# A chunk-select attention and gMLP kernel whose scheduler gets another length model, with the k copies as max(x,x) and the identity made first

## The chip, the core and the metric

The kernel runs on one core of a Trainium2 chip. The metric is the device time of one execution in microseconds (us). Five engines work side by side, each through its own list in order: TensorE (PE; its weight loads are PEld), VectorE (DVE), ScalarE (ACT), GpSimd (POOL) and SyncE (SP). Here GpSimd issues all loads and SyncE all stores and all crossbar transposes; a transfer then runs on the core's 16 DMA engines. An engine that waits for something holds up everything behind it in its list.

## The reference

Inputs are q, k, v of (4, 8, 768, 64) and the weights of one gated MLP. For every query the 6 best of 24 chunks of 32 keys are chosen by an upper bound, attention runs over these chunks, and the joined heads go through the MLP with a spatial mix:

```python
k_min, k_max = min and max of k over each chunk of 32 keys
ub = sum(maximum(q * k_min, q * k_max))        # per query and chunk, causal
top_chunks = argsort(ub)[-6:]
scores = q @ k.T / 8, masked to top_chunks and causal
x = softmax(scores) @ v                        # heads joined: (4, 768, 512)
h = relu(x @ w_in);  u, v = h[..., :512], h[..., 512:]
v_n = (v - mean(v)) / sqrt(var(v) + 1e-6)
v_s = w_spatial @ v_n + b_spatial
out = (u * v_s) @ w_out
```

## The kernel before

The work is cut into 16 pairs of heads (4 batches of 4 pairs) and, after each batch's four pairs, the MLP of that batch in 6 tiles of 128 rows. Matmuls run on f16 with f32 sums in 8 banks of PSUM.

For a pair: GpSimd loads kp, qs (two halves) and vt (L321, L325, L328), casting to f16. TensorE transposes k (L376) and ScalarE copies it to kT. VectorE makes chunk minima and maxima of kT (L382, L385, L388: a tree) into kmm, spreads them into km (L395: on VectorE for pairs 0 and 1, on GpSimd after) and copies kT into kh (L403, four copies of 64x384 that change between the two partition halves). q is transposed (L410) and its positive and negative parts are rq (L412, L415); L425 multiplies rq by km, which gives the bounds. VectorE masks them (L433), finds the 8 largest (L441) and writes "not chosen" flags into spare columns of qs (L447). qs with its flags is transposed into a: by TensorE (L461, copied by L464) for pairs 0 to 4, by a crossbar transpose that SyncE issues (L452) from pair 5 on. The flags meet large negative rows in kh (the pattern ex, made from identity at L292 and copied by six L300 copies into three kh buffers), so that one score matmul (L486) also masks. ScalarE takes exp (L493), GpSimd zeroes the upper triangle from pair 4 on (L501), L510 multiplies by v, L518 and L522 normalize into x. x is transposed into xT: on TensorE (L538, L541) for pairs 0 to 3 and the last, by SyncE (L530) for the others.

For a tile of the MLP: v = L557 on xT, ScalarE's relu (L561), bn_stats and bn_aggr on VectorE (L563, L565), normalization (L574); u = L584 and L588; the spatial sum L598 over six tiles of v; g = L602; g transposed to gT by SyncE (L606) in batches 0 to 2 and by TensorE (L613, L615) in batch 3; L620 multiplies by w_out; ScalarE copies to o (L623) and SyncE stores it (L625).

Nothing of this order is written by hand. Every step is an op with an engine, a length (occ), a time after which others see its result (vis), a key and the buffers that it reads and writes. Schedule.run plays the ops through: it always takes the op that can start first by its model, with the smaller key where two tie, gives it a PSUM bank and notes it. That sequence is then issued, so the numbers in the model decide each engine's list. Loads pass one model server (loads), everything else only its engine. The two lines on loads:

```python
loads = max(loads, t + 0.6) + o.load
o.seen = loads + 1.7
```

Of the kernel before, what the change touches and what calls it, by code (L numbers as in the profile page):

```python
# [14 lines left out]
P = 128  # L15
# [42 lines left out]
class Op:  # L58
    __slots__ = ("eng", "occ", "vis", "emit", "key", "take", "drop", "deps", "left", "users", "start", "end",
                 "seen", "load", "n", "tag")  # L60


class Schedule:
# [31 lines left out]
    def run(self):  # L95
        free = {e: 0.0 for e in ("PE", "ACT", "DVE", "POOL", "SP")}
# [19 lines left out]
        while left:  # L116
# [48 lines left out]
MM = 1 / 2400.0  # L165

# [15 lines left out]
def kernel(  # L182
# [93 lines left out]
    def const_ops():  # L276
        s.op("DVE", 0.1, 0.2, lambda: nc.vector.memset(identity, 0.0), -100, w=["identity"])
        s.op("POOL", *pool(P), c_identity, -90, w=["identity"], r=["identity"])
# [19 lines left out]
        for j in range(len(kh_r)):  # L298
            for hi in range(2):
# [33 lines left out]
    def weight_ops(key):  # L333
# [22 lines left out]
    def spatial_ops(key):  # L356
        for so in range(NQT):
# [7 lines left out]
            s.op("DVE", 0.474, 0.58, lambda so=so, bk=bk: nc.vector.tensor_copy(wsT[:, so, :], bk.f16[:, 0:S]),  # L365
# [306 lines left out]
```

## Time and profile before

| what | us |
|---|---|
| time, median of 2 runs | 238.43 (237.49 and 239.36) |
| the profiled execution's own time | 237.0 |
| its span | 235.0 |
| TensorE busy | 194.6 (83%) |
| VectorE busy | 171.9 (73%) |
| ScalarE busy | 144.6 (62%) |
| GpSimd busy | 102.9 (44%) |
| software DMA queue (loads), share of 16 engines | 71.7% |
| hardware DMA queue (stores, transposes) | 32.5% |

The span runs from the first to the last instruction that the profiler saw; the profiled execution's own time is 2 us longer. Busy time of TensorE counts each matmul to the end of its result, so it says little about how full it is; where it stood is read from its idle times and from what ended them. The share of a whole span mixes stages with different limits, so the rows below are taken by stretch.

### The profile page before, as it was taken

Reading aid. Unit: us, or ns where it says so; the run is one execution under the profiler, and the core shown is the slowest. Engines: PE = TensorE matmul, PEld = TensorE weight load, DVE = VectorE, ACT = ScalarE, POOL = GpSimd, SP = SyncE. Lnnn points to the kernel's source line nnn. Section 1 sums busy time; section 2 is a strip of 40 time slices with the busy share of each in tenths; the row PEclk is TensorE's granted clock in tenths of the full one; section 3 lists DMA queues with packets and bytes.
Section 4 is the critical chain, followed back from the end, with each engine's and each line's share of the span. In section 5 each row is a group of like instructions: output and inputs, shape, how many; then the busy total and the mean of one; then the engine's idle time right before and its main releaser. Section 6 shows DMA issues by size and latency. Waiting matters only on the chain. (4 is left out here: it accounts for less than half of the span.)

```text
span 235.0 us, 5366 instructions
## 1 busy us (share of the span) xinstructions
PE 194.6 (83%) x1910; PEld 115.8 (49%) x1910; DVE 171.9 (73%) x604; ACT 144.6 (62%) x297; POOL 102.9 (44%) x184
## 2 busy tenths in 40 slices
PE   0259889797999895794999987996999998699983
PEld 0146767576555453462655543564455554344541
DVE  4899999999899957278489994399996332276450
ACT  2117877767997833596588742797796847266111
POOL 8998579752836562194556452144310302000000
PEclk9999999999999999999799999999799999979999
DMA  9999999999893999999996979839512665100222
GB/s 60 122 150 148 155 174 189 177 134 109 60 137 35 135 175 157 230 129 109 109 162 57 96 164 143 208 134 134 79 27 42 106 181 168 45 0 0 80 101 89
DMA packets 117306, 27.68 MB, mean 118 GB/s; under 512 B 111904, under 2 KB 114208, under 8 KB 117280
## 3 DMA queue, kind: packets, MB, share of 16 engines
q0 software_dynamic: 77200, 12.19, 71.7%
q1 hardware_dynamic: 40080, 15.15, 32.5%
q8 instruction: 15, 0.25, 0.4%
q14 instruction: 11, 0.09, 0.1%
HBM read 24.38 MB, written 6.29 MB: 131 GB/s over the span
## 5 line engine op out<-in xcount | busy, mean ns | idle before, releaser
L493 ACT ACTIVATE e<-bank 128x512 f16<-128x512 f32 x192 | 93.0, 554 | 26.4 <-PE bank L486 13.6
L486 PE MATMUL bank<-a,kh 128*128 128x512 f16 (+3 forms) x256 | 58.2, 312 | 3.9 <-DVE a L464 2.1
L501 POOL TENSOR_SCALAR_AFFINE_SELECT e<-e 128x384 f16<-128x384 f16 x48 | 25.3, 529 | 69.2 <-ACT e L493 68.8
L598 PE MATMUL bank<-vn,wsT 128*128 128x512 f16 x144 | 37.2, 379 | 0.0
L623 ACT COPY o<-bank 128x512 f32<-128x512 f32 x24 | 14.0, 585 | 35.9 <-PE bank L620 34.2
L510 PEld LDWEIGHTS <-e 128*128 128x128 f16 x672 | 28.8, 98 | 10.8 <-POOL e L501 1.3
L510 PE MATMUL bank<-vt,e 128*128 128x65 f16 x672 | 32.4, 194 | 1.0 <-POOL e L501 0.6
L486 PEld LDWEIGHTS <-kh 128*128 128x128 f16 x256 | 23.0, 99 | 17.3 <-issue 3.6
L602 DVE SCALAR_TENSOR_TENSOR g<-bank,bcol,u 128x512 f16<-128x512 f32 x24 | 17.9, 748 | 17.4 <-PE bank L598 15.5
L557 PE MATMUL bank<-w_in,xT 128*128 128x512 f16 x96 | 27.7, 419 | 3.6 <-DMA xT<-x 3.0
L620 PE MATMUL bank<-w_out,gT 128*128 128x512 f16 x96 | 23.9, 380 | 7.6 <-DMA gT<-g 7.0
L325 POOL DMA_DIRECT2D qs<-in_q_dram x32 | 26.7, 848 | 2.3 <-DMA a<-qs 2.1
L584 PE MATMUL bank<-w_in,xT 128*128 128x512 f16 x96 | 24.3, 379 | 0.0
L403 DVE COPY kh<-kT 64x384 f16<-64x384 f16 x64 | 22.2, 347 | 1.2
L321 POOL DMA_DIRECT2D kp<-in_k_dram x16 | 17.0, 1064 | 9.7 <-PE bank L376 7.1
L561 ACT ACTIVATE vraw<-bank 128x512 f32<-128x512 f32 x24 | 14.0, 607 | 9.5 <-PE bank L557 9.3
L378 ACT COPY kT<-bank 128x768 f16<-128x768 f16 x16 | 13.1, 821 | 10.8 <-PE bank L376 10.0
L563 DVE BATCH_NORM_STATS2 st<-vraw 128x6 f32<-128x512 f32 x24 | 15.9, 682 | 4.8 <-ACT vraw L561 4.8
L518 DVE RECIPROCAL rec<-bank 128x6 f32<-128x6 f32 x32 | 6.0, 186 | 18.1 <-PE bank L510 17.9
L598 PEld LDWEIGHTS <-wsT 128*128 128x128 f16 x144 | 13.1, 97 | 11.9 <-issue 0.3
L522 DVE TENSOR_TENSOR x<-bank,rec 128x384 f16<-128x384 f32 x32 | 17.7, 553 | 0.6
L328 POOL DMA_DIRECT2D vt<-in_v_dram x16 | 16.5, 1034 | 3.3 <-PE bank L510 2.5
(59 smaller groups left out, 258.3 us busy)
## 6 DMA issues: line engine op xcount, KB each, us to landing
out_dram<-o SPq DMA_DIRECT2D x24, 256.0 KB, 2.3
kp<-in_k_dram POOLq DMA_DIRECT2D x16, 192.0 KB, 5.0
qs<-in_q_dram POOLq DMA_DIRECT2D x32, 96.0 KB, 4.9
vt<-in_v_dram POOLq DMA_DIRECT2D x16, 192.0 KB, 5.9
ws_raw<-in_moe_w_spatial_dram POOLq DMA_DIRECT2D x3, 384.0 KB, 8.5
w_in<-in_moe_w_in_dram POOLq DMA_DIRECT2D x4, 256.0 KB, 8.5
w_out<-in_moe_w_out_dram POOLq DMA_DIRECT2D x2, 256.0 KB, 8.3
gT<-g SPq DMA_TRANSPOSE x18, 2.5
```

The source lines that it names most:

```text
L325: s.op("POOL", 0.84, 0, lambda hi=hi, c0=c0: nc.gpsimd.dma_start(out=qs[:, :, hi, c0:c0 + D], in_=one(q, hi)), key + 0.1, w=[("qd", i % le ...
L403: nc.vector.tensor_copy(o, f)
L486: mm(bs.f32[:, col:col + n], lhsT=kh[:, hi, t * P:(t + 1) * P], rhs=af[:, q0 // P:(q0 + n) // P, :], start=True, stop=not dg)
L493: s.op("ACT", *act_cost(WIDTHS[g]), lambda g=g, bs=bs, e=e: nc.scalar.activation(out=e[:, BASES[g]:BASES[g] + WIDTHS[g]], in_=bs.f32[:, 0: ...
L501: nc.gpsimd.affine_select(out=o, in_=o, compare_op=Alu.is_ge, fill=0.0, base=0, channel_multiplier=-1, pattern=[[0, 3], [1, P]])
L510: mm(o[:, qi, :], lhsT=e[:, c:c + P], rhs=vt[:, hi, t, 0:D + 1], start=(part == 0 and n == 0), stop=(part == 1 and n == len(bl) - 1))
L522: nc.vector.tensor_tensor(x16[:, :, hi, :], in0=o[:, :, 0:D], in1=rec.to_broadcast([P, NQT, D]), op=Alu.mult)
L557: mm(bk.f32, lhsT=x[:, ko, t * P:(t + 1) * P], rhs=w_in_sb[:, ko, DH:DFF], start=(ko == 0), stop=(ko == NDO - 1))
L584: mm(bk.f32, lhsT=x[:, ko, t * P:(t + 1) * P], rhs=w_in_sb[:, ko, 0:DH], start=(ko == 0), stop=(ko == NDO - 1))
L598: mm(bk.f32, lhsT=wsT[:, si, t * P:(t + 1) * P], rhs=vn[:, si, :], start=(si == 0), stop=(si == NQT - 1))
L602: s.op("DVE", 0.61, 0.70, lambda t=t, bk=bk, g=g: nc.vector.scalar_tensor_tensor(out=g, in0=bk.f32, scalar=bcol[:, t:t + 1], in1=u_r[nu[t] ...
L620: mm(bo.f32, lhsT=gT[:, db, :], rhs=w_out_sb[:, db, :], start=(db == 0), stop=(db == KO - 1))
```

## The change

No arithmetic changes. The scheduler gets other numbers and rules:

- the engines start late by a little (free), a result is seen 0.25 later by another engine (LATE);
- an op with `load` passes the one DMA server, and now stores and crossbar transposes have a load too; a transfer of SyncE is seen 1.5 later than before (LATE_X);
- `slack`: a load can start only 3.0 after what it waits for, a store 4.0 (0.3 in the last batch), by the model. The chip's instruction waits as before; only its place in the list comes later;
- most lengths of VectorE are set anew, the kh copies from 0.16 to 0.28;
- the kh copies, and the km copies of pairs 0 and 1, are `tensor_tensor` max of x with x;
- the identity's key puts it behind the first load of GpSimd's queue.

```diff
-        free = {e: 0.0 for e in ("PE", "ACT", "DVE", "POOL", "SP")}
+        free = {"PE": 0.8, "ACT": 2.1, "DVE": 0.8, "POOL": 1.3, "SP": 0.8}
...
-                t = max(t, d.end if d.eng == o.eng == "PE" else d.seen)
-            ready[o.eng].append((o.key, o.n, t, o))
+                t = max(t, d.end if d.eng == o.eng == "PE" else d.seen if d.eng == o.eng else d.seen + LATE)
+            ready[o.eng].append((o.key, o.n, t + o.slack if o.deps else t, o))
...
-                loads = max(loads, t + 0.6) + o.load
-                o.seen = loads + 1.7
+                loads = max(loads, o.end) + o.load
+                o.seen = loads + 1.5 + (LATE_X if o.eng == "SP" else 0.0)
...
+LATE = 0.25
+LATE_X = 1.5
+LOAD_SLACK = 3.0
...
-        s.op("POOL", *pool(P), c_identity, -90, w=["identity"], r=["identity"])
+        s.op("POOL", *pool(P), c_identity, -100.99, w=["identity"], r=["identity"])
...
-                    (nc.vector if i < 2 else nc.gpsimd).tensor_copy(o, f)
+                    if i < 2:
+                        nc.vector.tensor_tensor(o, in0=f, in1=f, op=Alu.max)
+                    else:
+                        nc.gpsimd.tensor_copy(o, f)
...
-                    nc.vector.tensor_copy(o, f)
-                s.op("DVE", 0.16, 0.28, put, key + 3, r=[("kT", n2)], w=[("kh", nh, hi, par)])
+                    nc.vector.tensor_tensor(o, in0=f, in1=f, op=Alu.max)
+                s.op("DVE", 0.28, 0.40, put, key + 3, r=[("kT", n2)], w=[("kh", nh, hi, par)])
...
-            s.op("SP", 2.7, 4.7, lambda: nc.sync.dma_start_transpose(
+            s.op("SP", 1.5, 0, lambda: nc.sync.dma_start_transpose(
...
-                s.op("SP", 0.95, 3.0, lambda g=g, gT=gT: nc.sync.dma_start_transpose(out=gT, in_=g), kk,
-                     r=[("g", ng)], w=[("gT", ngt)])
+                s.op("SP", 1.25, 0, lambda g=g, gT=gT: nc.sync.dma_start_transpose(out=gT, in_=g), kk,
+                     r=[("g", ng)], w=[("gT", ngt)], load=0.55)
```

Every engine's list changes by this; the lines of the changed kernel lie 3 to 6 further down. Two places are shown.

VectorE's list at the start of the program before (kh0 to kh2 are the three kh buffers, t1 and t2 the tree, bank2 the bounds of pair 0):

```order
L300 COPY kh0_92<-ex_70 64x768
L382 TENSOR_TENSOR t10_95<-kT0_90 128x384 x2
L385 TENSOR_TENSOR t20_97<-t10_95 128x192 x2
L388 TENSOR_REDUCE kmm0_99<-t20_97 128x24 x2
L412 TENSOR_SCALAR rq0_103<-bank1_62 128x640
L395 COPY km0_101<-kmm0_99 64x2x3x4 x4
L415 TENSOR_SCALAR rq0_103<-bank1_62 128x640
L403 COPY kh0_92<-kT0_90 64x3x128 x4
L433 TENSOR_TENSOR bank2_63<-bank2_63,cmask_71 128x5x2x4
L300 COPY kh0_92<-ex_70 64x768
L441 MAX m80_105<-bank2_63 128x8 x10
L300 COPY kh1_93<-ex_70 64x768
```

The same place in the changed kernel, from the first kh<-ex copy on:

```order
L303 COPY kh0_92<-ex_70 64x768 x2
L293 MEMSET vt2_88 128x12x2
L283 MEMSET km1_102 128x48
L289 MEMSET eps_73 128x1
L303 COPY kh1_93<-ex_70 64x768 x2
L303 COPY kh2_94<-ex_70 64x768 x2
L276 MEMSET qs3_85 128x6x32
L277 MEMSET qs3_85 128x6x32
L293 MEMSET vt3_89 128x12x2
L385 TENSOR_TENSOR t10_95<-kT0_90 128x384 x2
L388 TENSOR_TENSOR t20_97<-t10_95 128x192 x2
L391 TENSOR_REDUCE kmm0_99<-t20_97 128x24 x2
```

All six copies of ex and the last memsets moved ahead of the first tree. Before, one stood ahead of it, one between mask and L441, one behind L441 and three behind the first L447.

SyncE's list in the MLP of batch 0 before (a is the transposed q of a pair, x the normalized output, o a store's tile):

```order
L530 DMA_TRANSPOSE xT1_122<-x162_120 128x6x128
L606 DMA_TRANSPOSE gT0_164<-g0_160 128x4x128
L606 DMA_TRANSPOSE gT1_165<-g1_161 128x4x128
L452 DMA_TRANSPOSE a1_108<-qs3_85 128x12x128
L625 DMA out_0_dram<-o0_170 128x512
L606 DMA_TRANSPOSE gT2_166<-g2_162 128x4x128
L530 DMA_TRANSPOSE xT1_122<-x160_118 128x6x128
L625 DMA out_0_dram<-o1_171 128x512
L606 DMA_TRANSPOSE gT3_167<-g3_163 128x4x128
L625 DMA out_0_dram<-o2_172 128x512
L606 DMA_TRANSPOSE gT4_168<-g0_160 128x4x128
```

And in the changed kernel:

```order
L612 DMA_TRANSPOSE gT0_164<-g0_160 128x4x128
L612 DMA_TRANSPOSE gT1_165<-g1_161 128x4x128
L536 DMA_TRANSPOSE xT1_122<-x162_120 128x6x128
L458 DMA_TRANSPOSE a1_108<-qs3_85 128x12x128
L612 DMA_TRANSPOSE gT2_166<-g2_162 128x4x128
L612 DMA_TRANSPOSE gT3_167<-g3_163 128x4x128
L612 DMA_TRANSPOSE gT4_168<-g0_160 128x4x128
L536 DMA_TRANSPOSE xT1_122<-x160_118 128x6x128
L631 DMA out_0_dram<-o0_170 128x512
L612 DMA_TRANSPOSE gT5_169<-g1_161 128x4x128
L458 DMA_TRANSPOSE a2_109<-qs0_82 128x12x128
```

The stores moved behind the transposes, because the L620 that make their tiles moved. How far is counted in TensorE's two lists: the matmul columns between the last L598 of a tile and the first L620 of the same tile, and between the last L510 of pair 7 and the second half of the first L557 of batch 1, in units of one 512-column matmul:

| tile | 0 | 1 | 2 | 3 | 4 | 5 |
|---|---|---|---|---|---|---|
| batch 0, before | 26.1 | 20.6 | 23.7 | 22.2 | 18.7 | 25.4 |
| batch 0, changed | 34.8 | 37.8 | 49.0 | 44.6 | 41.4 | 37.6 |
| batch 1, before | 19.9 | 28.1 | 19.6 | 24.9 | 29.9 | 19.9 |
| batch 1, changed | 31.6 | 30.8 | 31.0 | 36.9 | 37.6 | 31.5 |
| batch 2, before | 27.2 | 20.2 | 17.9 | 21.2 | 18.9 | 18.9 |
| batch 2, changed | 36.7 | 31.8 | 32.1 | 31.9 | 30.9 | 32.1 |

xT of pair 7: 17.9 before, 28.3 changed. From the K transpose of pair 11 to that of pair 14: 155.8 before, 46.6 changed.

## Rows read from the trace of the kernel before

**Rows 1.** Stretches in us: busy time (count) of each engine, clock, DMA share, GB/s.

```profile
0.00:20.00 20.00, 7.03 (x56) 5.28 (x57) 15.47 (x62) 4.10 (x6) 18.70 (x26) 1.00 1.84 116
20.00:80.00 60.00, 54.19 (x722) 38.25 (x720) 57.80 (x223) 47.13 (x99) 38.34 (x67) 1.00 1.44 132
80.00:115.00 35.00, 26.91 (x273) 15.94 (x272) 21.36 (x78) 21.15 (x43) 15.43 (x29) 0.97 1.42 157
```

**Rows 2.** The chain that ended last: start us, us, what.

```profile
215.57 2.59 PE bank L598 x12
```

**Rows 3.** Waits, TensorE: line waited for, us in total, times, longest.

```profile
PE bank L620 <- DMA gT<-g: 7.0, 8, 2.4
PE bank L557 <- DMA xT<-x: 3.0, 1, 3.0
PE bank L425 <- DVE x L522: 2.0, 1, 2.0
PE bank L425 <- POOL km L395: 1.6, 4, 0.8
```

**Rows 4.** Timeline, TensorE, 81 to 91: start us, us, what, [idle before <-releaser].

```profile
81.67 0.59 PE L598 MATMUL bank<-vn,wsT 128*128 128x512 f16 x2
...
90.53 0.82 PE L620 MATMUL bank<-w_out,gT 128*128 128x512 f16 x3 [2.42 <-DMA gT<-g]
```

**Rows 5.** Stretches of 5 us; columns as in rows 1, clock third from last.

```profile
110.00:115.00 5.00, 3.09 (x32) 2.35 (x33) 2.00 (x7) 2.20 (x5) 0.77 (x2) 0.82 1.63 154
115.00:120.00 5.00, 5.00 (x38) 2.52 (x37) 3.79 (x20) 2.48 (x6) 4.20 (x8) 0.84 1.14 91
...
165.00:170.00 5.00, 4.84 (x26) 2.35 (x25) 4.85 (x18) 4.06 (x8) 1.52 (x5) 0.72 0.60 84
```

**Rows 6.** Timeline, VectorE, 5 to 22 us.

```profile
7.23 0.63 DVE L382 TENSOR_TENSOR t<-kT 128x384 f16<-128x384 f16 x2 [0.75 <-ACT kT L378]
...
8.63 0.48 DVE L412 TENSOR_SCALAR rq<-bank 128x640 f16<-128x640 f16 x1
9.03 1.89 DVE L395 COPY km<-kmm 64x24 f16<-64x24 f16 x4
...
11.47 1.43 DVE L403 COPY kh<-kT 64x384 f16<-64x384 f16 x4
12.93 0.21 DVE L433 TENSOR_TENSOR bank<-bank,cmask 128x40 f32<-128x40 f32 x1
13.17 0.58 DVE L300 COPY kh<-ex 64x768 f16<-64x768 f16 x1
...
14.59 0.33 DVE L300 COPY kh<-ex 64x768 f16<-64x768 f16 x1
...
15.28 2.14 DVE L300 COPY kh<-ex 64x768 f16<-64x768 f16 x3
...
20.17 0.71 DVE L395 COPY km<-kmm 64x24 f16<-64x24 f16 x4
```

**Rows 7.** Single lines: count, ns min/median/max, first and last start.

```profile
L403 DVE COPY kh<-kT x64: 334/347/352, 11.5 to 171.9; 64x384 f16<-64x384 f16 x64
L382 DVE TENSOR_TENSOR t<-kT x32: 315/349/629, 7.2 to 162.8; 128x384 f16<-128x384 f16 x32
L385 DVE TENSOR_TENSOR t<-t x32: 210/248/574, 7.8 to 163.6; 128x192 f16<-128x192 f16 x32
```

**Rows 8.** Timeline, start, TensorE and GpSimd; last row: DMA issues, us to landing.

```profile
5.56 0.80 PE L376 MATMUL bank<-identity,kp 128*128 128x128 f16 x6 [5.56 <-POOL identity L269]
...
6.21 1.05 POOL L321 DMA_DIRECT2D kp<-in_k_dram  x1
...
kp<-in_k_dram POOLq DMA_DIRECT2D x16, 192.0 KB, 5.0
```

**Rows 9.** Timeline, GpSimd and VectorE, 158.5 to 161 us.

```profile
159.56 0.52 POOL L501 TENSOR_SCALAR_AFFINE_SELECT e<-e 128x384 f16<-128x384 f16 x1 [0.36 <-ACT e L493]
...
159.62 0.74 DVE L385 TENSOR_TENSOR t<-t 128x192 f16<-128x192 f16 x2
```

More of the change, by code (lines that the diff above doesn't have):

```diff
@@ L59 @@
     __slots__ = ("eng", "occ", "vis", "emit", "key", "take", "drop", "deps", "left", "users", "start", "end",
-                 "seen", "load", "n", "tag")
+                 "seen", "load", "slack", "n", "tag")
 class Schedule:
@@ L69, in __init__, with op @@
         self.writer, self.readers = {}, {}
-    def op(self, eng, occ, vis, emit, key, r=(), w=(), take=None, drop=None, load=0.0, tag=""):
+    def op(self, eng, occ, vis, emit, key, r=(), w=(), take=None, drop=None, load=0.0, slack=0.0, tag=""):
         o = Op()
         o.eng, o.occ, o.vis, o.emit, o.key, o.take, o.drop = eng, occ, vis, emit, key, take, drop
-        o.load, o.n, o.tag = load, len(self.ops), tag
+        o.load, o.slack, o.n, o.tag = load, slack, len(self.ops), tag
         deps = set()
@@ L93, in op, with run @@
         return o
-    def run(self):
-        free = {e: 0.0 for e in ("PE", "ACT", "DVE", "POOL", "SP")}
+    def run(self, fixed=None):
+        free = {"PE": 0.8, "ACT": 2.1, "DVE": 0.8, "POOL": 1.3, "SP": 0.8}
         ready = {e: [] for e in free}
@@ L364, in spatial_ops @@
                  take=bk, w=[bk])
-            s.op("DVE", 0.474, 0.58, lambda so=so, bk=bk: nc.vector.tensor_copy(wsT[:, so, :], bk.f16[:, 0:S]),
+            s.op("DVE", 0.48, 0.60, lambda so=so, bk=bk: nc.vector.tensor_copy(wsT[:, so, :], bk.f16[:, 0:S]),
                  key + 0.1 * so, r=[bk], w=[("wsT", so)], drop=bk)
@@ L381, in prep_ops @@
         for m, op in ((0, Alu.max), (1, Alu.min)):
-            s.op("DVE", 0.26, 0.38, lambda m=m, op=op: nc.vector.tensor_tensor(
+            s.op("DVE", 0.28, 0.40, lambda m=m, op=op: nc.vector.tensor_tensor(
                 t1[:, m], in0=kc[:, :, 0:16], in1=kc[:, :, 16:32], op=op), key, r=[("kT", n2)], w=[("t1", n2, m)])
@@ L434, in add_mask @@
                 [P, NQT - 1, 2, CPT]), op=Alu.add)
-        s.op("DVE", 0.17, 0.25, add_mask, key + 0.6, r=["cmask"], w=[bu])
+        s.op("DVE", 0.13, 0.27, add_mask, key + 0.6, r=["cmask"], w=[bu])
         def max8():
@@ L441, in max8 @@
                     nc.vector.max(m8[:, qi - 1, hi, :], bu.f32[:, c0:c0 + CPT * (qi + 1)])
-        s.op("DVE", 0.83, 0.92, max8, key + 0.6, r=[bu], w=[("m8", n2)])
+        s.op("DVE", 0.84, 0.98, max8, key + 0.6, r=[bu], w=[("m8", n2)])
         def select():
@@ L463, in prep_ops @@
                      take=ba)
-                s.op("DVE", 0.474, 0.58, lambda hi=hi, ba=ba: nc.vector.tensor_copy(
+                s.op("DVE", 0.48, 0.60, lambda hi=hi, ba=ba: nc.vector.tensor_copy(
                     a[:, :, hi, :], ba.f16[:, 0:S].rearrange("p (t c) -> p t c", c=P)), key + 0.7, r=[ba],
@@ L540, in attend_ops @@
                  take=bx)
-            s.op("DVE", 0.474, 0.58, lambda: nc.vector.tensor_copy(xT[:, hp, :], bx.f16[:, 0:S]), key + 6,
+            s.op("DVE", 0.48, 0.60, lambda: nc.vector.tensor_copy(xT[:, hp, :], bx.f16[:, 0:S]), key + 6,
                  r=[bx], w=[("xT", nxt, hp)], drop=bx)
@@ L562, in mlp_ops @@
                  kk, r=[bk], w=[("vr", nvr[t])], drop=bk)
[L563 removed]
+            s.op("DVE", 0.60, 0.74, lambda vraw=vraw, st=st: nc.vector.bn_stats(st, vraw), kk, r=[("vr", nvr[t])],
                  w=[("st", nst)])
[L565 removed]
+            s.op("DVE", 0.1, 0.22, lambda mv=mv, st=st, t=t: nc.vector.bn_aggr(mv[:, t % 3, :], st), kk,
                  r=[("st", nst)], w=[("mv", nmv, t % 3)])
@@ L624, in mlp_ops @@
                  w=[("o", no)], drop=bo)
-            s.op("SP", 0.1, 2.2, lambda t=t, o_sb=o_sb: nc.sync.dma_start(out=out[b, t * P:(t + 1) * P, :], in_=o_sb),
-                 kk + 0.3, r=[("o", no)], w=[("out", b, t)])
+            s.op("SP", 0.38, 0, lambda t=t, o_sb=o_sb: nc.sync.dma_start(out=out[b, t * P:(t + 1) * P, :], in_=o_sb),
+                 kk + 0.3, r=[("o", no)], w=[("out", b, t)], load=0.65, slack=4.0 if b < B - 1 else 0.3)
     const_ops()
```

46 lines of the change are left out of this document (22 added, 24 removed).

## The prediction

> **What bounds the kernel now.** I read the table of stretches first [rows 1]. From 20 to 80 us VectorE is busy 57.80 of 60 us while TensorE has 54.19: there VectorE sets the pace. From 80 to 115 us nothing is full (TensorE 26.91, VectorE 21.36 of 35 us), so waits set it; 13.6 us of VectorE lie idle there. TensorE's whole work is small against the span: 408,480 matmul columns stand in its list (counted from the order), and twelve 512-column matmuls that wait for nothing take 2.59 us [rows 2], so 0.216 us each and 172.3 us in all, of 235.0. The other 63 us are the start, waits, half clock and the end; the change can only win there.
>
> The list of waits names them [rows 3]: TensorE waited 7.0 us in 8 places at L620 for gT, which the crossbar makes from g; 3.0 us once at L557 for xT; 2.0 us once at L425 for the x of VectorE; 1.6 us in 4 places at L425 for the km copies of GpSimd. One case in full [rows 4]: the L598 sum of tile 2 of batch 0 ends at 82.26 us (81.67 + 0.59), its L620 starts at 90.53, 8.3 us later, of which the last 2.42 us TensorE stood.
>
> Half clock is the third loss: after the 3.0 us wait the granted clock is 0.82 and 0.84 in the stretches 110:115 and 115:120, and 0.72 in 165:170 after the wait at L425 [rows 5]; 1.00 is 2.4 GHz, so part of each stretch ran at 1.2. That is 5 x (0.18 + 0.16) = 1.7 us of TensorE lost once and 5 x 0.28 = 1.4 us the second time.
>
> **The change, part by part.** The arithmetic is unchanged; what changes is the order, and 72 VectorE copies that become max(x,x).
>
> *The start.* Six copies kh<-ex now stand before the first minima and maxima of k, not between the steps of the first selection. Five of them stood in that chain, for 0.58 + 0.33 + 2.14 = 3.05 us [rows 6]. All of it was on the path: VectorE does not rest from 7.23 us on. They take 0.33 to 0.71 us each (the last is the mean of three), 0.61 in the mean, while GpSimd, which issues the loads, is busy 18.70 of the first 20 us [rows 1]. The four km copies of pair 0 show the same: 1.89 us, and 0.71 us for pair 1 [rows 6]. As max(x,x) I give them 0.71, since the two-input L382 isn't stretched there (0.63 us for two, so 0.3 each, with twice the partitions): a gain of 1.18 us.
> Against it, all six and some memsets now stand between identity and the first L382. Identity ended TensorE's first wait at 5.56 [rows 8]; it now stands behind one load on GpSimd's queue instead of four, and an issue takes up to 1.05 us [rows 8], so with some 0.9 for each it comes at about 2.9. But kp0 is issued no earlier, and its 5.0 us to landing let TensorE start about when it did. From 2.9, ex and the memsets take some 1.8 us and the copies 6 x 0.33 to 6 x 0.71: the first L382 could start between 6.7 and 9.0 us, where it started at 7.23. At the mean it starts at 8.4, 1.15 us late. The K transpose of pair 1, now ahead of the first L425 on TensorE, waits for kp1, issued at 6.21 and landing 5.0 us later (the median) [rows 8]: about 11.2, when rq is done too, so it costs nothing; it would cost 1 us if rq came a us sooner. Start: 3.05 + 1.18 - 1.15 = 3.1 us won (bounds 2.4 and 4.2), and it carries to 80 us since VectorE is full.
>
> *The 64 kh copies as max(x,x).* They take 347 ns each, 334 to 352, never stretched; the nearest two-input row, L382 with the same 384 elements, has a median of 349 [rows 7]. So nothing by size. Four copies in a row take 1.43 us, 0.36 each, while the second of two L382 starts 0.27 after the first [rows 6]: if the new form overlapped like that, 64 x 0.09 = 5.8 us would be won. I don't take it, because the copies alternate between partition halves in either form and L382 doesn't.
> A rule of the Trainium skill speaks against this edit. First the rows: L382 and L385, which read two SBUF operands, reach 629 and 574 ns against medians of 349 and 248 [rows 7]; two L385 that take 0.74 us stand beside an L501 of GpSimd that was already running [rows 9]. The page SBUF — State Buffer, § Who interferes with whom, says that a VectorE instruction with two SBUF inputs contends with a GpSimd one that reads SBUF; the trace agrees (0.28 and 0.33 us extra), and by the page all 64 new copies are open to it. The kh copies of pairs 2 to 15 stand beside the km copies of GpSimd, 0.2 us each, and its L501, 0.52. If a quarter of the 64 lose 0.33 us that is 5.3 us; if none, 0. I take 1.5, since VectorE has room outside 20:80.
> Another page would price the edit higher. VectorE: DVE Perf Modes, § The perf-mode tier table, gives tensor_copy four elements a cycle and tensor_tensor two, by which 64 x 0.1 = 6.4 us (an estimate) would be lost; the 347 against 349 ns of the rows say that this copy isn't at the higher rate, and I go by them.
>
> *gT.* In every tile of batches 0 to 2 more matmul work stands between the L598 sum and the L620 that needs its gT (table of the change). Tile 2 of batch 0: 23.7 matmuls of 512 before, 49.0 now, so 10.6 us of work where 8.3 us were needed. Wherever the eight waits lie, the added work (batch 0: 1.9 to 5.5 us a tile; batch 1: 0.6 to 2.6) is about as long as a wait, of which the longest was 2.4. SP's list helps: stores and the next pair's transposes no longer stand between one gT and the next. The pair transposes that now come earlier stand on the same queue, so I take 6.0 of the 7.0 (bounds 3 and 7).
>
> *xT of pair 7.* 17.9 matmuls before, 28.3 now: 2.25 us more cover for a 3.0 us wait. I take 2.0, and half of the 1.7 us of clock (bounds 0 and 4.7).
>
> *Waits at L425.* Almost all transposes of k and q stand further ahead of their L425, and VectorE's minima and maxima of pairs 9 to 14 fill the idle 13.6 us of 80:115 instead of the full stretch behind it. Of 2.0 + 1.4 (clock) + 1.6 us I take 1.0 + 0.4 + 1.0 (bounds 0 and 5).
>
> *New waits.* The kp loads of pairs 13 and 14 are needed far earlier: from the K transpose of pair 11 to that of pair 14 TensorE had 156 matmuls of 512, now 46.6 (10.1 us), and a kp lands 5.0 us (median) after its issue [rows 8], the issue itself behind km copies on GpSimd's queue. I set 3.0 us against all new waits (bounds 0 and 10: two waits as long as the longest two before, with their half clock).
>
> **Sum.** 3.1 - 1.5 + 6.0 + 2.85 + 2.4 - 3.0 = 9.85 us. The profiled execution took 237.0 us, so 227.15; the median of the runs shown, 238.43, is 1.4 us above it, the faster run 237.49. I forecast 227.
>
> **Rivals.**
> *The waits only move.* TensorE gets past gT and then stands for VectorE, which is full in 20:80. Then only the start less the collisions (1.6 us) is kept: 235. For it: 57.80 of 60. Against it: the gT waits lie at 80:100 and 135:150, where VectorE idles.
> *Slower: VectorE late at batch 1.* In VectorE's list three trees of minima and maxima (1.40 us each, from 7.23 to 8.63), two selections (1.4 us each without the copies in between), nine kh copies (0.36), four rq (0.4) and one x (0.6) now stand ahead of the first bn_stats of batch 1 that stood behind it [rows 6], 12.4 us; TensorE comes to that batch only 4.1 us of matmul work later. If loads come too late for VectorE to do them in the idle of 80:115, the second matrix sum of batch 1 waits up to 12.4 us and half clock follows (1.7): 227 + 14.1 = 241. It decides from 10 us on; below that the kernel stays faster. Against it: 13.6 us idle suffice, and the K transposes concerned come 5 to 30 us of work earlier.
> *The new copies collide.* By the SBUF page's rule taken at its worst in the VectorE-bound stretch: 28 copies of pairs 1 to 7, 0.33 us each, 9.2 us less the 1.5 counted: 234.7. Against it: only 0.2 us GpSimd copies stand beside most of them.
> *More is won:* no new waits, both clocks back, copies that overlap: 218 or less.
>
> **Chances.** Forecast 0.62 (219 to 233.5), waits move 0.17, late VectorE 0.09, collisions 0.06, more won 0.06. What this kernel's measurement tells from no change is about 2%, 4.8 us: under 233.7 counts as faster. That holds for the forecast, for more won and for half of the collisions: 0.71; within 2% waits move and the rest: 0.20; slower 0.09. The range 219 to 236 leaves out 0.06 below and about 0.13 above.
>
> **What would show it.** Right: five kh<-ex copies gone from 13 to 17.5 us; km of pair 0 at about 0.7; the first score matmul a microsecond or more earlier; the wait for gT under 1 us in sum, for xT under 1; granted clock near 1.00 in all 5 us stretches until 200; VectorE busier in 80:115. Wrong: the kh copies over 0.40 us on average; a wait of TensorE at the K transposes for kp; bn_stats of batch 1 the last thing that the batch-1 sum waits for.

## The result, and the profile after

The changed kernel takes 218.38 us (two runs, 218.29 and 218.48) against 238.43: a ratio of 0.916, 95% interval 0.900 to 0.932. The profiled execution took 218.29 us with a span of 216.2 (before: 237.0 and 235.0), so the traces differ by 18.8 us. That is faster, as forecast, but below the range of 219 to 236, and 8.6 us below the forecast of 227. Some executions of a kernel take over 1.5% longer than its fastest, at a lower granted clock: the times of the experiments below are medians of all executions, while their ratios go by the fast ones.

The stretches of the changed kernel, with the columns of [rows 1] (busy time and count of TensorE, its weight loads, VectorE, ScalarE, GpSimd, then clock, DMA share, GB/s):

```profile
0.00:20.00 20.00, 8.67 (x76) 6.68 (x77) 17.50 (x75) 4.75 (x7) 18.80 (x27) 1.00 1.84 116
20.00:80.00 60.00, 54.00 (x721) 38.32 (x720) 56.65 (x219) 47.64 (x99) 39.29 (x68) 1.00 1.44 130
80.00:115.00 35.00, 30.77 (x337) 18.39 (x336) 32.95 (x131) 25.95 (x52) 22.75 (x46) 1.00 1.72 187
115.00:170.00 55.00, 54.61 (x520) 31.46 (x519) 41.87 (x142) 45.02 (x98) 20.08 (x40) 1.00 1.05 126
170.00:200.00 30.00, 28.10 (x201) 14.31 (x197) 14.89 (x33) 17.89 (x38) 3.13 (x6) 1.00 0.29 81
```

VectorE still fills 20:80, but now also 80:115 (32.95 of 35 us where it had 21.36), and from 115 to 170 TensorE stands 0.4 us in all. The granted clock is 1.00 everywhere to 200 us.

TensorE's waits in the changed kernel, as in [rows 3] (in us: total, times, longest):

```profile
PE bank L379 <- DMA kp<-in_k_dram: 8.2, 2, 5.2
PE bank L431 <- POOL km L401: 3.3, 2, 2.3
PE bank L416 <- DMA qs<-in_q_dram: 1.3, 2, 1.1
PE bank L467 <- DVE qs L453: 1.2, 1, 1.2
...
PE bank L492 <- DMA a<-qs: 0.8, 1, 0.8
```

There is no row for the crossbar's gT or for xT any more (7.0 and 3.0 us before), none of 2 us for VectorE, and the two waits for kp lie before 11 us.

VectorE's start in the changed kernel, against [rows 6]:

```profile
3.84 1.05 DVE L303 COPY kh<-ex 64x768 f16<-64x768 f16 x2
...
5.91 1.79 DVE L303 COPY kh<-ex 64x768 f16<-64x768 f16 x3
...
8.16 0.33 DVE L385 TENSOR_TENSOR t<-kT 128x384 f16<-128x384 f16 x1
...
9.93 0.70 DVE L399 TENSOR_TENSOR km<-kmm 64x24 f16<-64x24 f16 x4
...
11.18 1.45 DVE L409 TENSOR_TENSOR kh<-kT 64x384 f16<-64x384 f16 x4
12.66 0.21 DVE L439 TENSOR_TENSOR bank<-bank,cmask 128x40 f32<-128x40 f32 x1
```

Where the 18.8 us were won is read by counting: the matmul columns in TensorE's rows are summed in order, and the start of the matmul at the same sum is taken in both traces (in units of one 512-column matmul, of 797.8 in all; which matmul is taken at a sum moves a row by up to 0.4 us).

| units done | before, us | changed, us | won so far | what lies in the step before |
|---|---|---|---|---|
| 24 | 22.64 | 21.65 | 1.0 | start |
| 72 | 36.59 | 34.22 | 2.4 | |
| 96 | 42.55 | 42.30 | 0.3 | a new wait of 2.3 us for km at 42.3 |
| 215 | 73.90 | 70.79 | 3.1 | VectorE full |
| 359 | 117.92 | 110.69 | 7.2 | MLP of batch 0, xT of pair 7 |
| 526 | 160.36 | 148.25 | 12.1 | MLP of batch 1 |
| 550 | 170.09 | 154.26 | 15.8 | L425 of pair 14 |
| 669 | 196.34 | 180.66 | 15.7 | MLP of batch 2 |
| 717 | 212.16 | 193.47 | 18.7 | end of pair 15, start of the last MLP |
| end | 235.0 | 216.2 | 18.8 | |

### The profile page after: what moved, and what is told of

It is laid out like the page before. It is cut to its first block, busy times and chain, and to the rows that moved or that the text cites. A ratio compares the mean times of both kernels' runs of the same rounds, so it can differ in the third digit from the quotient of the medians.

```text
span 216.2 us, 5372 instructions
## 1 busy us (share of the span) xinstructions
PE 187.7 (87%) x1910; PEld 114.7 (53%) x1910; DVE 169.5 (78%) x604; ACT 144.8 (67%) x297; POOL 104.1 (48%) x184
## 4 chain that ended last, share of the span: by engine, by line
PE 59%; DVE 23%; DMA 8%; issue 4%; ACT 3%; POOL 1%; POOLq 0%; ACTq 0%; DVEq 0%
PE bank L604 12%; PE bank L492 11%; PE bank L590 8%; PE bank L563 8%; PE bank L626 7%; PE bank L516 7%; DMA vt<-in_v_dram 5%; DVE kh L409 4%; DMA a<-qs 3%; DVE m L447 3%; ACT e L499 2%; DVE t L385 2%; DVE x L528 1%; DVE rq L418 1%; DVE vn L580 1%
## 5 line engine op out<-in xcount | busy, mean ns | idle before, releaser
L492 PE MATMUL bank<-a,kh 128*128 128x512 f16 (+3 forms) x256 | 57.3, 310 | 3.7 <-DMA a<-qs 0.8
L507 POOL TENSOR_SCALAR_AFFINE_SELECT e<-e 128x384 f16<-128x384 f16 x48 | 26.2, 545 | 57.2 <-ACT e L499 56.3
L604 PE MATMUL bank<-vn,wsT 128*128 128x512 f16 x144 | 38.1, 379 | 0.4 <-DVE vn L580 0.4
L516 PE MATMUL bank<-vt,e 128*128 128x65 f16 x672 | 31.5, 193 | 1.3 <-POOL e L507 0.5
L492 PEld LDWEIGHTS <-kh 128*128 128x128 f16 x256 | 22.2, 99 | 18.1 <-issue 4.5
L608 DVE SCALAR_TENSOR_TENSOR g<-bank,bcol,u 128x512 f16<-128x512 f32 x24 | 17.9, 747 | 12.4 <-PE bank L604 12.1
L409 DVE TENSOR_TENSOR kh<-kT 64x384 f16<-64x384 f16 x64 | 23.6, 369 | 2.8 <-PE bank L492 1.4
L626 PE MATMUL bank<-w_out,gT 128*128 128x512 f16 x96 | 24.5, 379 | 0.8 <-DVE gT L621 0.7
L563 PE MATMUL bank<-w_in,xT 128*128 128x512 f16 x96 | 24.3, 379 | 0.4 <-DVE xT L547 0.4
L590 PE MATMUL bank<-w_in,xT 128*128 128x512 f16 x96 | 23.6, 379 | 0.0
L604 PEld LDWEIGHTS <-wsT 128*128 128x128 f16 x144 | 13.0, 98 | 10.9
L401 POOL COPY km<-kmm 64x24 f16<-64x24 f16 x56 | 12.4, 222 | 11.9 <-DVE kmm L391 9.5
```

The costliest lines, as they stand in the source:

```text
L409: nc.vector.tensor_tensor(o, in0=f, in1=f, op=Alu.max)
L492: mm(bs.f32[:, col:col + n], lhsT=kh[:, hi, t * P:(t + 1) * P], rhs=af[:, q0 // P:(q0 + n) // P, :], start=True, stop=not dg)
L507: nc.gpsimd.affine_select(out=o, in_=o, compare_op=Alu.is_ge, fill=0.0, base=0, channel_multiplier=-1, pattern=[[0, 3], [1, P]])
L516: mm(o[:, qi, :], lhsT=e[:, c:c + P], rhs=vt[:, hi, t, 0:D + 1], start=(part == 0 and n == 0), stop=(part == 1 and n == len(bl) - 1))
L563: mm(bk.f32, lhsT=x[:, ko, t * P:(t + 1) * P], rhs=w_in_sb[:, ko, DH:DFF], start=(ko == 0), stop=(ko == NDO - 1))
L590: mm(bk.f32, lhsT=x[:, ko, t * P:(t + 1) * P], rhs=w_in_sb[:, ko, 0:DH], start=(ko == 0), stop=(ko == NDO - 1))
```

## The experiments

All times are in us; the ratio with its 95% interval is to the kernel before on the same chip, whose medians were 238.3 (e1 to e4), 238.7 (e5 to e8), 238.4 (e9 to e12), 239.1 (e13, e14) and 238.5 (e15, e16). From the km copies on, the lines of e8, e13, e14 and e16 lie 3 further down than those of the kernel before, and the lines of e2 lie 3 further up than those of the changed kernel.

| run | kernel | time | ratio |
|---|---|---|---|
| e1 | before, gT late | 227.1 | 0.945 (0.934 to 0.956) |
| e2 | changed, all copies tensor_copy | 218.0 | 0.915 (0.910 to 0.920) |
| e3 | changed, LATE 0.26 | 219.4 | 0.921 (0.915 to 0.927) |
| e4 | changed, gT as before | 228.6 | 0.959 (0.953 to 0.965) |
| e5 | before, gT of batch 0 late | 233.7 | (none; 230.1 and three runs of 233.7 to 233.8) |
| e6 | before, gT of batch 1 late | 232.5 | 0.973 (0.966 to 0.981) |
| e7 | before, gT of batch 2 late | 235.6 | 0.986 (0.980 to 0.992) |
| e8 | before, start | 236.9 | 0.989 (0.982 to 0.996) |
| e9 | before, gT and xT late | 225.2 | 0.954 (0.945 to 0.963) |
| e10 | changed, kh copies tensor_copy | 217.8 | 0.922 (0.912 to 0.932) |
| e11 | e10, LATE 0.30, LATE_X 2.5 | 217.5 | 0.922 (0.917 to 0.928) |
| e12 | e10, LATE 0.32, LATE_X 3.0 | 220.6 | 0.936 (0.928 to 0.943) |
| e13 | e9 and start | 229.3 | 0.960 (0.955 to 0.966) |
| e14 | e13, LATE, a late | 226.9 | 0.950 (0.946 to 0.954) |
| e15 | changed, LOAD_SLACK 0 | 223.3 | 0.935 (0.927 to 0.942) |
| e16 | e13 and load slack | 224.5 | 0.939 (0.931 to 0.948) |

### One number: gT

```diff
-                s.op("SP", 0.95, 3.0, lambda g=g, gT=gT: nc.sync.dma_start_transpose(out=gT, in_=g), kk,
+                s.op("SP", 0.95, 5.5, lambda g=g, gT=gT: nc.sync.dma_start_transpose(out=gT, in_=g), kk,
```

> The kernel before with one number changed: the crossbar transposes of g are seen 5.5 instead of 3.0 us after their start by the model, so that the L620 that need them are issued later; nothing else of the change. By the lists, the matmul work between a tile's last L598 and its L620 grows: summed over the six tiles, what is missing to 8.3 us falls from 20.3, 19.0 and 22.9 us (batches 0, 1, 2) to 7.6, 5.3 and 6.9; the K transposes of pairs 13 and 14 and the start stay where they were. Theory (the cover removes the waits): TensorE's wait at L620 for gT falls from 7.0 to about 2 us, the time by about 5 us, to 233 (ratio 0.979). Rival (the waits only move to another producer): within 1 us of the kernel before. If the waits at the two places of batch 1 and 3 where the clock fell stay, the granted clock there still falls.

(Cover is the matmul work between a tile's last L598 and its first L620; what is missing is counted against the 8.3 us between the two in [rows 4], summed over the six tiles of a batch.)

Measured: 227.1, more than twice the gain that was expected (11.2 us by the medians, 13 by the ratio, whose interval allows 10 to 16).

```profile
PE bank L620 <- DMA gT<-g: 0.2, 1, 0.2
```

The wait for gT is down to 0.2 us, but the 2.0 us at L425 and the half clock are gone too: the profiled execution has 1.00 in every stretch up to 220 us. So making gT late is worth more than the gT waits. The reverse is e4, which gives the changed kernel the old numbers of gT (0.95, 3.0, no load):

> The changed kernel with the model numbers of the crossbar transposes of g as before (0.95, seen after 3.0, no DMA server). By the lists the missing cover of gT is 16.8, 18.0 and 17.7 us (changed kernel 1.1, 6.7 and 7.6; kernel before 20.3, 19.0 and 22.9), and the K transpose of pair 14 is late as in the run with LATE 0.26 (107.6 us of work). Theory: 5 to 6 us of waits for gT return, and 3.7 us at pair 14: 227 to 228. Rival (gT's waits were only a sign of VectorE or loads being late, and the gain is the start and the earlier loads): 219 to 222.

Measured: 228.6, 10.2 us above the changed kernel. The waits for gT are back, and with them a clock of 0.69 in 95:100 and 0.75 in 140:145.

```profile
PE bank L626 <- DMA gT<-g: 7.5, 5, 2.2
```

Two theories were left: A, that a gT wait is worth its own length, and B, that a late L620 also fills other waits, as filler: matmul work that TensorE can do while another engine is behind. The next three make gT late for one batch each (5.5 if b is that batch, else 3.0).

> As the run that makes the transposes of g late for all batches, but only for batch 0: by the lists the missing cover of batch 0 falls from 20.3 to 7.6 us, batches 1 and 2 stay (16.6 and 22.5). The kernel before waits 4.3 us for gT in batch 0, and 3.0 us for xT of pair 7 with half clock behind it (1.7 us). Theory A (a gT wait is worth its own length): 4 us, 234.3. Theory B (a late L620 also fills other waits of the same stretch, and the clock with them): the xT wait shrinks and its half clock goes as well, 6 us, 232.3.

> Only the transposes of g of batch 1 seen late: missing cover of batch 1 from 19.0 to 6.6 us, the others unchanged. The kernel before waits 2.7 us for gT there, later 2.0 us at the L425 of pair 14 with half clock behind it (1.4 us). Theory A: 2.7 us, 235.6. Theory B: the L620 that now stand beside pair 13 and 14 fill the wait at L425, so 2.0 and 1.4 us go as well: 6 us, 232.3.

> Only the transposes of g of batch 2 seen late; the lists are the same up to the middle of batch 2, GpSimd's list altogether. TensorE waits for no gT in batch 2 of the kernel before. Theory A (a gT wait is worth its own length): nothing to win, within 0.5 us of 238.3. Theory B (late L620 are filler): at the end of pair 15, where TensorE waits for exp, x and xT (2.6 us in all) and its clock falls behind that (0.66 in 205:210, 1.7 us), L620 groups now stand between these steps; 1.3 us of idle time and the 1.7 us of half clock go, 3 us, 235.3.

Measured: 5.0, 6.2 and 3.1 us won by the medians. Batch 0 decides nothing: three of its runs won 5 us and one over 8; in its trace the half clock behind the xT of pair 7 is gone, but the wait itself fell only from 3.0 to 2.4 us. Batches 1 and 2 are B's (0.973 and 0.986, where A allowed 0.989 and 1.000, both outside the intervals). Batch 2 is the clearest, since TensorE waited for no gT there. Before, the stretches behind pair 15 (columns as above):

```profile
200.00:205.00 5.00, 2.94 (x36) 1.72 (x35) 1.31 (x3) 1.25 (x3) 0.52 (x1) 1.00 0.14 52
205.00:210.00 5.00, 5.00 (x16) 1.90 (x15) 3.05 (x8) 2.82 (x5) 0.00 (x0) 0.66 0.00 0
```

In e7, TensorE's timeline (start, us, what, and in brackets the idle time before and its releaser) and the same stretch:

```profile
202.81 0.51 PE L538 MATMUL bank<-identity,x 128*128 128x128 f16 x6 [0.95 <-DVE x L522]
203.15 0.38 PE L557 MATMUL bank<-w_in,xT 128*128 128x512 f16 x1
204.04 1.25 PE L557 MATMUL bank<-w_in,xT 128*128 128x512 f16 x5 [0.51 <-DVE xT L541]
205.13 1.03 PE L620 MATMUL bank<-w_out,gT 128*128 128x512 f16 x4
...
205.00:210.00 5.00, 5.00 (x25) 2.26 (x24) 4.58 (x12) 4.05 (x10) 0.00 (x0) 1.00 0.14 52
```

The list is the same up to batch 2. One L620 group that stood ahead of the last L510 of pair 15 is now done behind its xT and the others a step later; the wait of 0.7 us that an L620 had there is gone, and the clock is 1.00 instead of 0.66. By the count used above, 2.6 us are won from 669 to 717 units, where B has them. (The clock of a single trace is not a matter of order alone: e7 has 0.66 in 90:95, where its order is that of before and before has 1.00.) In e6 two L620 of batch 1 stand just ahead of the L425 of pair 13, and the L425 of pair 14, which had waited 1.98 us for VectorE, waits no more:

```profile
153.92 1.03 PE L620 MATMUL bank<-w_out,gT 128*128 128x512 f16 x4
...
156.06 1.03 PE L620 MATMUL bank<-w_out,gT 128*128 128x512 f16 x4
156.92 0.41 PE L425 MATMUL bank<-km,rq 128*128 128x48 f16 x10
...
161.62 0.41 PE L425 MATMUL bank<-km,rq 128*128 128x48 f16 x10
```

There, from 526 to 550 units, e6 has won 4.3 us. An L620 whose gT has landed needs nothing more of VectorE. Issued as soon as the old model thought gT was there, it waited for the crossbar and was then used up; issued later, it gives VectorE time where VectorE is behind. B fits e1, e4, e6 and e7 and is read from the traces at two places, pair 14 and the end of pair 15; that all of the extra gain is filler isn't shown. Other changes of order alone move the time by as much as e7 (e11 and e12 below, 3.1 us).

### The early K transposes

```diff
-LATE = 0.25
+LATE = 0.26
```

> The changed kernel with LATE 0.26 instead of 0.25. Such a step changes little of the order but one place: the K transpose of pair 14 stands behind 105.4 us of matmul work instead of 75.1, and its minima and maxima on VectorE behind 124.7 us of VectorE's work instead of 114.4, while its L431 stays at 111.3 (110.2). The cover of gT is about the same (missing to 8.3 us: 1.9, 6.9 and 9.0 us against 1.1, 6.7 and 7.6). Theory (the early K transpose of pair 14 is what removed the wait and the half clock before batch 2): a wait of about 2 us at the L431 of pair 14 and a stretch of half clock behind it return, 3.7 us slower, 222. Rival (that part of the gain has another cause): within 1 us of the changed kernel.

Measured: 219.4, its interval overlapping that of e2, which has the changed order; no wait of 2 us at the L431 of pair 14. The expected 3.7 us did not come, so the early K transpose of pair 14 was not what removed that wait.

### The copies

> The changed kernel with all 72 copies (64 of kT into kh, 8 of kmm into km on VectorE) as tensor_copy again; the order of every engine's list is the same. Theory: the form of the kh copies is worth nothing by size (347 against 369 ns in the two traces, 64 x 0.022 = 1.4 us of VectorE, most of it hidden), and the km copies of pair 0 take 1.9 us again instead of 0.70, on the path of the first selection, 1.2 us: in sum 0 to 1.2 us slower than the changed kernel, 218.4 to 219.6. Rival 1 (the max copies overlap better): 5 us slower, 223. Rival 2 (the max copies collide with GpSimd): 2 to 5 us faster, 214 to 216.

Measured: 218.0, as the changed kernel. Duration rows (count, ns min/median/max, first and last start), first the changed kernel, then two rows of VectorE's timeline in e2:

```profile
L409 DVE TENSOR_TENSOR kh<-kT x64: 332/353/616, 11.2 to 152.6; 64x384 f16<-64x384 f16 x64
...
L399 DVE TENSOR_TENSOR km<-kmm x8: 154/167/170, 9.9 to 16.8; 64x24 f16<-64x24 f16 x8
```

```profile
9.91 1.20 DVE L398 COPY km<-kmm 64x24 f16<-64x24 f16 x4
...
16.75 1.68 DVE L398 COPY km<-kmm 64x24 f16<-64x24 f16 x4
```

So both effects are there and small: as max(x,x) the km copies take 0.70 us for four and not 1.20 or 1.68, and the kh copies lose 1.4 us over all 64 (mean 369 ns on the page after, 347 as tensor_copy on that before), most of it in five that took 492 to 616 ns, four of them beside an L507 of GpSimd. In sum they cost or win no time that can be told. The Trainium skill's page SBUF — State Buffer, § Who interferes with whom, says that a copy can take the port pair shared with GpSimd, while a tensor_tensor with two SBUF inputs meets only GpSimd's reads: both signs agree, though the kh copies as tensor_copy were never stretched (352 ns at most in [rows 7]). By the rate table of the Trainium skill's page VectorE: DVE Perf Modes, § The perf-mode tier table, e2 should have saved VectorE much more than that; 353 against 347 ns says that this copy does not run at the table's higher rate. The edit that takes the better form of each, against the changed kernel:

```diff
-                    nc.vector.tensor_tensor(o, in0=f, in1=f, op=Alu.max)
+                    nc.vector.tensor_copy(o, f)
```

> The changed kernel with the 64 kh copies as tensor_copy, the 8 km copies as max(x,x); the same order. The max copies of kh took 369 ns in the mean and up to 616, the tensor_copy 347 and at most 352; the km copies of pairs 0 and 1 took 0.70 us as max and 1.20 and 1.68 as tensor_copy. Theory: each half takes its better form; up to 1.4 us of VectorE for the kh copies, of which what lies in the full stretch (some 28 of 64 copies) counts, 0.6 us: 217.8, against 218.4 (all max) and 218.0 (all copy). Rival: no difference beyond 0.3 us.

Measured: 217.8, six runs from 216.1 to 219.5; 0.6 us can't be told in that.

### The start, the xT, and what takes the start's gain back

e8 is the kernel before with the identity's new key and all 72 copies as max(x,x).

> The kernel before with the identity early (key -100.99) and all 72 copies as max(x,x); the length model is the old one. Four of the six copies of ex move ahead of the first tree, two stay in the chain of the first selection. The missing cover of gT becomes 20.8, 22.9 and 22.5 us (20.3, 19.0 and 22.9 before). Theory: the km copies of pair 0 take 0.70 us (1.9) and those of pair 0's chain lose one and a half us of ex copies, the start gains 1.5 to 2.5 us, the cover of batch 1 costs up to 1: 236 to 237. Rival 1 (the start gain is lost again to VectorE or loads before 80 us): 238.3. Rival 2 (the start is the large part of the gain): 232 or less.

Measured: 236.9, as expected: 1.8 us won by the medians and 2.6 by the ratio, with an interval of 1 to 4. Its trace stands 2.8 us ahead at 215 units, near the 3.1 that the changed kernel has won there. e9 makes gT and xT late and leaves the start as it was.

```diff
-            s.op("SP", 1.4, 3.4, lambda: nc.sync.dma_start_transpose(
+            s.op("SP", 1.4, 5.9, lambda: nc.sync.dma_start_transpose(
```

> The kernel before with two numbers changed: the crossbar transposes of g seen after 5.5 instead of 3.0 us and those of x after 5.9 instead of 3.4. Missing cover of gT 7.6, 5.9 and 6.8 us (changed kernel 1.1, 6.7 and 7.6); the work between the last L510 of pair 7 and its L557 is 6.0 us (3.9 before, 6.1 in the changed kernel, 4.6 with gT alone). Theory: the 2.1 us of waiting for xT that were left with gT alone go as well: 225 (227.1 with gT alone). Rival (what xT waited for was the end of pair 7 itself, which only shows under another name): 227.

Measured: 225.2; no wait for xT is left. Two numbers of the model give more than half of the 20 us (0.954, where the changed kernel has 0.916). But xT adds nothing to e1 that can be told: by the ratio e9 (0.954) is no faster than e1 (0.945), and TensorE's waits turn up elsewhere (for a, 1.8 us, and below). e13 puts the start on top:

> The run with the transposes of g and x late, and besides the identity early and the 72 copies as max(x,x). By the lists the cover stays as without the start (missing 7.5, 5.9 and 6.8 us for gT; 6.2 us ahead of the L557 of pair 7). Theory (the start gain of about 3 us carries to the end where the waits behind it are covered): 222, against 225.2 without the start. Rival (VectorE or loads take it back in any case): 225.

Measured: 229.3, and the theory fell: no gain over e9 that can be told (by the medians 4 us lost, though the intervals overlap). By the count used above the start had won 3.4 us at 215 units, and 0.1 was left at 454. The waits show where it went: in e13 GpSimd stands at loads, with e and km behind them in its list, and TensorE waits for these. GpSimd's and TensorE's waits, then one case from 116 to 119 us:

```profile
POOL qs L325 <- DMA a<-qs: 13.8, 5, 4.8
```

```profile
PE bank L513 <- POOL e L504: 7.8, 7, 2.7
...
PE bank L428 <- POOL km L398: 4.9, 9, 1.2
```

```profile
116.79 0.82 POOL L325 DMA_DIRECT2D qs<-in_q_dram  x1 [4.23 <-DMA a<-qs]
117.62 0.53 POOL L504 TENSOR_SCALAR_AFFINE_SELECT e<-e 128x384 f16<-128x384 f16 x1
```

```profile
118.21 0.27 PE L513 MATMUL bank<-vt,e 128*128 128x65 f16 x3 [2.72 <-POOL e L504]
```

A load of qs may overwrite its buffer only when the transpose into a has read it. The load waits 4.23 us for that, the zeroing of e behind it is late, and TensorE stands 2.72 us. In the changed kernel GpSimd waits 1.1 us for a in one place, and TensorE 0.5 us for e. These waits of GpSimd did not come with the start, though. They are there as soon as gT is late (14.6 us in e1, 2.1 before), and in e9, without the start, GpSimd's and TensorE's are:

```profile
POOL qs L325 <- DMA a<-qs: 12.3, 5, 3.8
```

```profile
PE bank L510 <- POOL e L501: 3.6, 7, 1.3
PE bank L425 <- POOL km L395: 3.4, 6, 1.3
```

With the start TensorE's two waits grow from 7.0 to 12.7 us while GpSimd's hardly grows. e14 tests LATE and a late a against this, with the load rules of before:

```diff
-                t = max(t, d.end if d.eng == o.eng == "PE" else d.seen)
+                t = max(t, d.end if d.eng == o.eng == "PE" else d.seen if d.eng == o.eng else d.seen + 0.25)
...
-            s.op("SP", 2.7, 4.7, lambda: nc.sync.dma_start_transpose(
+            s.op("SP", 2.7, 7.2, lambda: nc.sync.dma_start_transpose(
```

> As the run beside it, and every result seen 0.25 us later by another engine (LATE), and the transposes of qs into a seen 7.2 instead of 4.7 us after their start; the load server, the slack and all lengths are those of before. Missing cover 0.0, 2.2 and 3.7 us; the K transpose of pair 13 moves from 105.5 to 72.8 us of work, as in the changed kernel (74.4). Theory (lateness between engines is the rest): 218.5 to 219.5, the changed kernel's time, with the waits for e, km and a half as long. Rival (the load server, slack or lengths carry the rest): 221 to 222.

Measured: 226.9. The waits for e fell (1.5 us), yet neither number came true: a new wait for a itself, of 3.1 us, is followed by half clock (the clock had been down before it too, 0.77 in 100:105).

```profile
110.09 1.03 PE L489 MATMUL bank<-a,kh 128*128 128x512 f16 x2 [3.12 <-DMA a<-qs]
```

```profile
110.00:115.00 5.00, 4.26 (x18) 1.65 (x19) 2.18 (x7) 2.28 (x4) 3.92 (x8) 0.50 1.72 168
```

The slack of the loads (they are placed 3 us later in GpSimd's list) was then tried from both sides. e15 takes it from the changed kernel; e16 adds it alone to e13.

```diff
-LOAD_SLACK = 3.0
+LOAD_SLACK = 0.0
```

> The changed kernel with LOAD_SLACK 0 instead of 3.0. The cover of gT stays (missing 2.6, 4.6 and 7.6 us against 1.1, 6.7 and 7.6). Theory (slack keeps loads that must wait out of GpSimd's way): GpSimd's waits at loads of qs for a rise from 1.1 to more than 6 us, TensorE's waits for e and km with them, 222 to 224. Rival (slack is not what matters, the order of the other engines is): 218 to 220.

```diff
-            ready[o.eng].append((o.key, o.n, t, o))
+            ready[o.eng].append((o.key, o.n, t + (3.0 if o.deps and o.load else 0), o))
```

> The run with late transposes of g and x and the start (229.3), and a load with dependences placed 3.0 us later. Missing cover of gT 3.4, 5.5 and 8.8 us (7.5, 5.9, 6.8). Theory: GpSimd's waits at loads of qs fall from 13.8 to under 4 us, TensorE's for e from 7.8 to under 3, and the start gain stays: 222 to 224. Rival: 228 to 230.

Measured: 223.3 and 224.5, both inside what the theory gave. In e15 the loads that wait are others than expected, mostly those of vt; GpSimd's waits and TensorE's:

```profile
POOL vt L331 <- PE bank L516: 6.2, 5, 1.8
POOL qs L328 <- DMA a<-qs: 3.9, 2, 3.2
POOL kp L324 <- PE bank L379: 3.7, 2, 2.4
```

```profile
PE bank L431 <- POOL km L401: 3.8, 3, 2.7
PE bank L516 <- POOL e L507: 3.5, 3, 1.8
```

Part of the price of e15 is half clock behind the km wait of 2.7 us (0.66 in 40:45, where the changed kernel has 1.00 behind one of 2.3). In e16 the wait of 13.8 us is gone:

```profile
POOL qs L325 <- DMA a<-qs: 0.6, 1, 0.6
```

So the slack is worth some 5 us on the side of the changed kernel (223.3 less 218.4 by the medians, 4.6 by the ratios of e15 and e2). On the other side it is 4.9 by the medians (229.3 less 224.5) and 5.0 by the ratios, but only some 3 against the two fastest runs of e13 (226.1 and 228.4). Slack on e9 without the start was not run, so whether it gives the start's gain back or would win as much without it isn't shown.

### More of the same

> As the run before it, with LATE 0.30 and LATE_X 2.5 (0.25 and 1.5 in the changed kernel): missing cover of gT 0.0, 1.0 and 3.8 us (1.1, 6.7, 7.6), 8.1 us of work ahead of the L557 of pair 7 (6.1), the K transposes of pairs 13 and 14 early as in the changed kernel. In the changed kernel no wait for gT or xT is left, so by the theory more cover wins nothing of itself; what it could win is filler at the end of pair 15 (1.9 us of waits there): 216.5 to 218. Rival (more lateness pushes L620 behind where they are needed, the output tail grows): 219 to 221.

> As the run before it, with LATE 0.32 and LATE_X 3.0: missing cover 0.0, 0.1 and 0.7 us, 8.2 us ahead of the L557 of pair 7. Theory and rival as there; if cover is no longer what limits, this and the run before differ by less than 1 us and by order alone.

Measured: 217.5 and 220.6. More lateness wins nothing that can be told (e11), and still more costs: the interval of e12 lies above that of e11. The two differ by 3.1 us, not by less than 1, so the order still matters where cover doesn't. No version here is clearly better than the changed kernel; 217.5 to 218.4 are one group.

## Why the prediction was off

The direction held, and the size of the start. The gT term failed, and two things that won time stand in no term. Taking the steps in their order, with the won time of the table above:

- **The start**: 3.1 us forecast, 3.1 won at 215 units. The first L385 starts at 8.16 (8.4 forecast), km of pair 0 takes 0.70 us (0.71), and the K transpose of pair 1 ends its wait for kp at 10.96 (11.2) and delays little, since rq is done at 11.15. e8 and e13, which have the start without the rest, stand 2.8 and 2.9 us ahead of before at 215 units. That the gain simply carries on from there was too easy: in e13 it is gone by 454 units, where TensorE waits for GpSimd.
- **The copies**: 1.5 us forecast, 1.4 us of VectorE measured. The agreement is luck: the 1.5 was picked between 0 and 5.3, and not a quarter of the copies was stretched but five of 64. It should have been no term, since e2 and e10 show no cost in time that can be told.
- **gT**: here the step failed. I gave 6.0 us, a wait at its own length, with the added work only as cover. The change of that one number gave 11 to 13 us (e1), and taking it back cost 10.2 (e4). Late L620 are also filler for VectorE's waits at pair 14 and pair 15, where no gT was waited for (e6, e7). In the table the steps from 215 to 526 units won 9.0 us, against 6.85 forecast for them (6.0, 2.85 and 1.0, less 3.0). The 2.85 of these for xT are not shown as a term: late xT on top of late gT won nothing that can be told (e9 against e1).
- **Waits at L425**: 1.4 us forecast for pair 14 (1.0 and 0.4 of clock), 3.7 won from 526 to 550 units, and the cause was another: not the K transpose of pair 14 further ahead (e3) but L620 as filler (e6).
- **Half clock**: of the rows of before, up to 5 x (0.18 + 0.16 + 0.28 + 0.34) = 4.8 us of TensorE were lost (less where it stood idle); I took 0.85 and 0.4 of it and missed the stretch 205:210 wholly. In the trace of the changed kernel no stretch before 215 us is below 1.00. The step from 669 to 717 units, 3.0 us, stands in no term of mine.
- **New waits**: 3.0 us forecast, put on kp of pairs 13 and 14. No K transpose waits there. What came is a wait for km of 2.3 us at 42.3, made good by 71 us, as it would be if VectorE, full there, sets the pace.
- **The slack of the loads**: a part of the change to which I gave no price. It is worth some 5 us, by keeping waiting loads out of the way of e and km on GpSimd (e15, e16). Late gT brings these waits about (e1, e9), so without the slack the whole change would have won about 5 us less.

By the table the sum was short by 2.15 us from 215 to 526 units, 2.3 at pair 14, 3.0 at the end of pair 15 and the 1.5 of the copies: 8.95 us, all that lies between the 18.8 us won and the 9.85 of the sum.

Of the rivals, the one in which more is won came true, at the 218 that it gave, by the clocks and not by copies that overlap. I gave it 0.06 because I took its parts as independent bits of luck. They had one cause at least in part: with the late gT alone the waits at pair 14 and the half clock went together (e1). That short waits are safe is not shown: before, 205:210 fell to 0.66 behind waits of 0.49, 0.95 and 0.51 us.

What stays open: e16, with late gT and xT, the start and the slack, stands at 224.5; the remaining 6 us to the changed kernel are in LATE, the server for stores and transposes, the stores' slack and the new lengths together. Its trace has a wait of 2.8 us for a at 109.74 and a clock of 0.66 in 110:115 and 0.71 in 190:195, where the changed kernel waits 0.8 us for a in all and keeps 1.00. Run e14 shows that LATE and a late a without the slack don't give it; the parts were not told apart further. Whether single steps add can't be told: gT by batches won 5.0 + 6.2 + 3.1 = 14.3 us one by one and 11 to 13 together, which the spread of the runs allows. The start won 2.8 us at 215 units by itself, and on e9 nothing at the end that can be told.

## What to carry to other kernels

Where an in-order engine waits for a transfer, look not only at the wait but at what the early instruction could have filled later: work that needs nothing of the engine that is behind is worth keeping for the places where one waits for it. Count the half clock behind a wait with the wait where a trace shows it, and ask whether several waits have one cause before giving the case that all of them go a small chance. A load that must wait for its buffer is an instruction like any other in its queue; place it late enough that it doesn't hold up the compute behind it.

## What the runs showed of the hardware

- A transpose by the crossbar can take far longer than its median: that of a is 4.5 us from issue to landing before (5.8 at most), but in e14 the a issued at 99.17 was still awaited by the L489 at 110.09, 10.9 us later, with a DMA share of 2.34 in 105:110. What held it up was not tested.
- TensorE's clock fell behind waits of very different length: to 0.50 in 110:115 of e14 (that is 1.2 GHz) behind one of 3.12 us, to a mean of 0.66 in 205:210 of before behind three of 0.95 us and less. One wait of 2.31 us at 42.3 in the changed kernel left it at 1.00, while one of 2.71 us at the same place in e15 gave 0.66 in 40:45. What tells these apart was not tried.
- Four copies of 64x24 in a row took 0.70 us as max(x,x) for both pairs, while GpSimd was issuing loads. As tensor_copy they took 1.89 us (before), 1.20 and 1.68 us (e2) beside such issues, but 0.71 us at 20.17 in before, where GpSimd stood until its next load at 20.75.
